# Gelu split into four operations, and P.V accumulated in PSUM with the score fill ahead of it

## The chip, the cores and the metric

The kernel runs on one core of one Trainium2 chip. Its engines are TensorE (PE in the profile; its weight loads are PEld), VectorE (DVE), ScalarE (ACT), GpSimd (POOL) and SyncE (SP), which here only issues DMAs. Each runs its own list of instructions in order, and the lists are tied together by semaphores: an instruction waits until a counter has reached a value. The metric is the time of one execution on the device in microseconds; lower is better.

## The reference

Input is one sequence of S = 2048 rows and D = 512 columns in bf16. Four residual blocks follow each other, with the same weights for both of a kind: A, B, A, B, each on the layernorm of x.

```
A: q = (x @ wq) as 32 heads of 16; k = x @ wk; v = x @ wv     # one k and v for all heads
   p = softmax(q k^T / 4);  o = p v;  out = concat(o) @ wo
B: z = gelu_tanh(x @ w_in)                                     # 1792 wide
   z1 = z[..., :896];  z2 = layernorm(z[..., 896:])
   g = w_sp @ z2 + b_sp                                        # 2048 x 2048 mixing of rows
   out = (z1 * g) @ w_out
x = x + A(ln(x));  x = x + B(ln(x));  x = x + A(ln(x));  x = x + B(ln(x))
```

gelu_tanh(u) is 0.5 u (1 + tanh(0.798 u + 0.0357 u^3)).

## The kernel before

x stays in SBUF (tile `X`) through all four layers. All the instructions are put into one list per engine by `K.op(engine, fn, waits, inc)`, in the order in which the Python code calls it; that order is the only scheduler there is. The waits given to one call stand in front of that instruction, so what comes later on that engine is queued behind them.

**Start** (lines 182 to 246). SP issues the loads of x (four), wq, wk, wv, wo (semaphore wA), then w_in and w_out (wB) and b_sp. DVE zeroes and fills padded copies of wq, wk and wv, sets `V_aug` to zero with a column of ones per head slot (that column gives the softmax denominator), and then starts the first layernorm (`bn_stats` L275, `bn_aggr` L276).

**Layer A** (`layer_A`). Work is cut into units: (qc, hg, kt) is one chunk of 512 query rows, one group of four heads and one tile of 128 keys. There are 4 x 8 x 16 = 512 units; the 16 units of one (qc, hg) are called a group. A unit has four blocks, one per head, of 128 keys x 512 queries. Three blocks at a time form a fill: `emit_fill(i)` puts three score matmuls (L754) into three of six PSUM banks, and `emit_exp(i)` (L773) lets ScalarE take exp of all three banks in one instruction of 128x1536 into `P_ring`, a ring of 12 blocks. So there are 683 exps in a layer. `emit_pv(u)` (L793) multiplies four blocks of `P_ring` with `V_aug` into one bank, `pv_bank`, each head into its own 32 partitions. In the kernel before, every unit's product is complete in itself, and DVE adds it into `acc_sb` in SBUF: a copy for the first of a group (L814), adds for the next 14 (L816), and the last add writes `oT_bf` (L818). P.V of the next unit waits for that add, since there is one bank.

Beside it runs a list of side tasks that share one bank, one per step of the main loop: layernorm transposes and K/V projections at the start, 30 Q projections (L487) and, in layer 0, 32 tasks that transpose w_sp; after each group a finalize task (four transposes of `oT_bf`, L663, then a reciprocal and a scaling on DVE, L668 and L673); after each query chunk two transposing tasks into `onT` (L697) and four Wo tasks (L715), which add to `X` (L720). `emit_side_pe` puts the next task's TensorE part into the list, and `emit_side_dve` its DVE part.

**Layer B** (`layer_B`). After layernorm and transposes, 60 items go through TensorE: first 32 for z2 (16 row tiles x 2 halves of 448 columns, L899), then 28 for z1 (four chunks x seven tiles of 128x512, L904), each four matmuls into one of four banks (`slot = k % 4`). `step_gelu` turns each bank with one `Gelu_apprx_tanh` on ScalarE (L933) into bf16 in `z2n` or `z1c`. For z2, DVE takes `bn_stats` (L937) and `bn_aggr` (L940) and, six items later, normalizes the row tile in place (L952); POOL computes the reciprocal root (L941, L943). Then per chunk of 512 rows: the mixing matmuls (L1009) read all of `z2n`, DVE adds b_sp (L1019) and multiplies with z1 (L1025), and the last matmuls with `w_out_r` (L1041) are added to `X` (L1047).

Of the kernel before, what the change touches and what calls it, by code (L numbers as in the profile page):

```python
# [5 lines left out]
FP32 = mybir.dt.float32  # L6
BF16 = mybir.dt.bfloat16
# [10 lines left out]
NF1 = 7  # L18
# [86 lines left out]
def bass_interleave_layers__grouped_kv_mqa__mixer_gmlp__prompt_kernel(  # L105
# [89 lines left out]
    with ExitStack() as wst:  # L195
# [23 lines left out]
        def dve_memset(ap, val, waits=()):  # L219
            return K.op("dve", lambda e: e.memset(ap, val), waits=waits, inc=S_dve)  # L220
# [19 lines left out]
                wv_rep[:].rearrange("p kd (g r) -> p kd g r", r=32)[:, :, :, 0:DH],  # L240
                wv_nat[:, :, None, :].to_broadcast([P, KD, 4, DH])),
            waits=[(S_dve, v0), wA], inc=S_dve)
        v0 = dve_memset(V_aug[:], 0.0)
        w_prep_v = dve_memset(V_aug[:].rearrange("p t (c r) -> p t c r", r=32)[:, :, :, DH], 1.0,
                              waits=[(S_dve, v0)])
# [86 lines left out]
    def layer_A(layer_idx, x_waits, do_wspt=False):  # L332
# [9 lines left out]
        acc_sb = K.sb([P, QC], FP32, lst, name="acc_sb")  # L342
# [435 lines left out]
        def emit_pv(u):  # L778
            qc, hg, kt = units[u]
            kc = kt // CT  # L780
            while kc not in V_ready:
                progressed = emit_side_pe()
                progressed = emit_side_dve() or progressed
                assert progressed, "V block task missing"
            wl = [(S_exp, exp_base + iu(u) + 1), V_ready[kc], prologue_done]
            if u >= 1:
                wl.append((S_acc, acc_base + u))

            def pe_fn(e):
                ins = None  # L790
                for j in range(4):
                    slot = (4 * u + j) % 12
                    ins = e.matmul(pv_bank[32 * j:32 * j + 32, 0:QC], V_aug[:, kt, 32 * j:32 * j + 32], P_ring[:, slot, :],  # L793
                                   tile_position=(0, 32 * j), start=True, stop=True)
                return ins
            K.op("pe", pe_fn, waits=wl, inc=S_pv)

        def emit_acc(u):
            qc, hg, kt = units[u]
            grp = u // NT  # L800
            par = grp % 2
            wl = [(S_pv, pv_base + u + 1)]
            if u >= 1:
                wl.append((S_acc, acc_base + u))
            last = (kt == NT - 1)
            if last and grp >= 2:
# [4 lines left out]
            if NT == 1:  # L811
                fn = lambda e: e.tensor_copy(oT_bf[:, par, :], pv_bank[:, 0:QC])
            elif kt == 0:
                fn = lambda e: e.tensor_copy(acc_sb[:], pv_bank[:, 0:QC])  # L814
            elif not last:
                fn = lambda e: e.tensor_tensor(acc_sb[:], pv_bank[:, 0:QC], acc_sb[:], ALU.add)  # L816
            else:
                fn = lambda e: e.tensor_tensor(oT_bf[:, par, :], pv_bank[:, 0:QC], acc_sb[:], ALU.add)  # L818
            v = K.op("dve", fn, waits=wl, inc=S_acc)
            if last:  # L820
                side_urgent.append(make_fin_task(qc, hg, par, v))
                if hg == 7:
                    qpar = qc % 2
                    nhalf = (NQT + 1) // 2
                    for half in range(nhalf):
                        side_urgent.append(make_ont_task(qc, half, qpar))
                    for qt in range(NQT):
                        side_urgent.append(make_wo_task(qc, qt, qpar))

        pending_pv = {}  # L830
        for u in range(U):
# [3 lines left out]
            emit_fill(1)  # L835
        for i in range(NI):
            emit_exp(i)
            for u in pending_pv.get(i, []):
                emit_pv(u)
                emit_acc(u)  # L840
            if i + 2 < NI:
                emit_fill(i + 2)
            emit_side_pe(allow_bg=(i % SIDE_PERIOD == 0))
            emit_side_dve()
        for i in range(NI, NI + 8):
            for u in pending_pv.get(i, []):
                emit_pv(u)
                emit_acc(u)
# [12 lines left out]
    def layer_B(layer_idx, x_waits):  # L861
# [12 lines left out]
        z2n = K.sb([P, NT, FH], BF16, lst, name="z2n")  # L874
        z1c = K.sb([P, NF1, S], BF16, lst, name="z1c")
        NSLOT = 4
        st2 = K.sb([P, NT, 2, 6], FP32, lst, name="st2")
        mv2 = K.sb([P, NT, 2], FP32, lst, name="mv2")
        veps2 = K.sb([P, NT], FP32, lst, name="veps2")
        rstd2 = K.sb([P, NT], FP32, lst, name="rstd2")  # L880

        items = []
        for t in range(NT):
# [28 lines left out]
            _, tc, ft = it  # L912
            return z1c[:, ft, tc * TCW:(tc + 1) * TCW]

        st = {"pe": [None] * NIT, "a0": [None] * NIT}
# [11 lines left out]
        def step_gelu(k):  # L927
            it = items[k]
            slot = k % NSLOT
            bk = bank32(slot)  # L930
            n = item_N(it)
            oap = out_ap(it)
            st["a0"][k] = K.op("act", lambda e, bk=bk, n=n, oap=oap: e.activation(  # L933
                oap, bk[:, 0:n], ACTF.Gelu_apprx_tanh), waits=[(S_pe, st["pe"][k])], inc=S_act)
            if it[0] == "z2":
                _, t, h = it
                v1 = K.op("dve", lambda e, t=t, h=h: e.bn_stats(st2[:, t, h, :], z2n[:, t, h * 448:(h + 1) * 448]),  # L937
                          waits=[(S_act, st["a0"][k])], inc=(S_dloc if h == 1 else None))
                if h == 1:
                    vm[t] = K.op("dve", lambda e, t=t: e.bn_aggr(mv2[:, t, :], st2[:, t, :, :]), waits=[(S_dloc, v1)], inc=S_dve)  # L940
                    vp1 = K.op("pool", lambda e, t=t: e.tensor_scalar(veps2[:, t:t + 1], mv2[:, t, 1:2], LN_EPS, None,  # L941
                                                                       op0=ALU.add), waits=[(S_dve, vm[t])], inc=S_ploc)
# [25 lines left out]
        z2n_all = (S_dve, max(vz2n))  # L968
# [16 lines left out]
        for tc in range(NTC):  # L985
# [9 lines left out]
            for ft in range(NF1):  # L995
# [8 lines left out]
                def pe_g(e, ft=ft, bk=bk, wb=wb, first_g=first_g):  # L1004
                    ins = None
                    for sti in range(NT):
                        if first_g:
                            e.wait_ge(S_dve.h, vz2n[sti])
                        ins = e.matmul(bk[:, 0:TCW], z2n[:, sti, ft * 128:(ft + 1) * 128], wspT[:, wb, sti, :],  # L1009
                                       start=(sti == 0), stop=(sti == NT - 1))  # L1010
                    return ins
                if first_g:
                    wl = [w_ for w_ in wl if w_ is not z2n_all]
                    K.waited["pe"][id(S_dve)] = max(K.waited["pe"].get(id(S_dve), 0), vz2n[NT - 1])
# [15 lines left out]
            for tt in range(NTT):  # L1030
                t = tc * NTT + tt
                yb = tt % 2
                bk = bank32(6 + yb)
                wl = [(S_dve, vh[NF1 - 1]), w_prep, wB]
                if y_bank_free[yb] is not None:
                    wl.append((S_dve, y_bank_free[yb]))

# [60 lines left out]
```

## Time and profile before

| | us |
|---|---|
| median of 9 runs | 2534.62 (2532.68 to 2535.91) |
| the profiled execution | 2536.26 |
| its span, first to last instruction | 2534.2 |
| busy: PE, ACT, DVE, POOL | 1875.5, 1983.3, 1096.0, 48.5 |
| exps of layer 0, first start to last end | 46.1 to 1045.6 |
| first MLP, gelu stage (L899, L904) to first mixing matmul | 1095.9 to 1147.5 |
| exps of layer 2 | 1307.4 to 2301.8 |
| second MLP, the same stage | 2352.0 to 2403.7 |

A timeline line gives start, duration, engine, source line, operation, output<-input, shapes and how often it follows itself; in brackets stands how long the engine was idle before it and what ended that. Independent instructions on one engine overlap a little, so that the distance between two starts is less than a duration. Busy PE is not PE at its peak: TensorE's clock is gated, and the column PEclk (or the seventh column of the windows) tells what share of it was granted. A line of the windows gives, for one stretch, its length and then busy time and count for PE, PEld, DVE, ACT and POOL, the clock, the DMA share and GB/s.

### The profile page before, as it was taken

The page shows a single profiled execution, that of the slowest core. Times are in us where ns is not written, and L with a number is a line of the kernel's source. Part 1 is how long each engine was busy: PE and PEld are TensorE (multiplying, and loading weights), DVE is VectorE, ACT ScalarE, POOL GpSimd, SP SyncE. Part 2 cuts the span into 40 slices and gives each one's busy share as a digit, 9 for nine tenths or more (in the row PEclk, how much of TensorE's full clock was granted, in tenths as well). Part 3 has the DMA queues.
Part 4 walks back from the last instruction along what each step waited for, and adds up shares of the span by engine and source line. Part 5 has one row for each costly group of instructions (what it writes and reads, how often), then busy time and mean ns, then how long its engine had stood idle before and what let it go on. Part 6 is the DMA issues. An engine that isn't in the chain of part 4 may idle for free.

```text
span 2534.2 us, 29104 instructions
## 1 busy us (share of the span) xinstructions
PE 1875.5 (74%) x11232; PEld 547.5 (22%) x11232; DVE 1096.0 (43%) x1818; ACT 1983.3 (78%) x1490; POOL 48.5 (2%) x95
## 2 busy tenths in 40 slices
PE   3878777777777777579958777777777777774899
PEld 1223111111111111144422111111111111111444
DVE  5665433343334333463366434333433343334533
ACT  2999999999999999540039999999999999993500
POOL 0000000000000000020000000000000000000200
PEclk9986555555555555589979655555555555555999
DMA  3035000000000000201100000000000000002020
GB/s 119 1 90 152 9 1 1 1 1 1 1 1 1 1 1 1 67 1 34 34 0 1 1 1 1 1 1 1 1 1 1 1 1 1 1 1 66 1 83 17
DMA packets 60088, 43.98 MB, mean 17 GB/s; under 512 B 34864, under 2 KB 57264, under 8 KB 59952
## 3 DMA queue, kind: packets, MB, share of 16 engines
q1 hardware_dynamic: 59952, 42.11, 5.6%
q8 instruction: 92, 1.51, 0.2%
q14 instruction: 44, 0.36, 0.0%
HBM read 31.62 MB, written 10.49 MB: 17 GB/s over the span
## 4 chain that ended last, share of the span: by engine, by line
PE 49%; DVE 21%; ACT 21%; issue 8%; POOL 1%; DMA 0%; SPq 0%; ACTq 0%; DVEq 0%
PE ps_all L793 21%; ACT P_ring L773 21%; DVE acc_sb L816 14%; PE ps_all L1009 8%; PE ps_all L754 7%; PE ps_all L899 2%; PE ps_all L1041 2%; PE ps_all L904 2%; PE ps_all L715 2%; DVE ln_stats L275 2%; DVE oT_bf L818 1%; PE ps_all L663 1%; DVE acc_sb L814 1%; PE ps_all L301 1%; PE ps_all L487 1%
## 5 line engine op out<-in xcount | busy, mean ns | idle before, releaser
L773 ACT ACTIVATE P_ring<-ps_all 128x1536 bf16<-128x1536 f32 (+1 forms) x1366 | 1910.0, 1452 | 286.6 <-PE ps_all L754 254.9
L816 DVE TENSOR_TENSOR acc_sb<-ps_all,acc_sb 128x512 f32<-128x512 f32 x896 | 618.4, 690 | 910.2 <-PE ps_all L793 908.9
L793 PE MATMUL ps_all<-P_ring,V_aug 128*32 128x512 bf16 x4096 | 595.9, 569 | 464.9 <-ACT P_ring L773 258.6
L754 PE MATMUL ps_all<-qT_pad,kT_rep 32*128 32x512 bf16 x4096 | 779.1, 568 | 27.2 <-ACT P_ring L773 13.3
L793 PEld LDWEIGHTS ps_all<-P_ring,V_aug 128*32 128x32 bf16 x4096 | 128.6, 100 | 925.8 <-ACT P_ring L773 888.7
L754 PEld LDWEIGHTS ps_all<-qT_pad,kT_rep 32*128 32x128 bf16 x4096 | 141.2, 98 | 581.1 <-issue 416.4
L1009 PE MATMUL ps_all<-wspT,z2n 128*128 128x512 bf16 x896 | 194.7, 379 | 1.5 <-issue 1.5
L933 ACT ACTIVATE z2n<-ps_all 128x448 bf16<-128x448 f32 x64 | 34.8, 543 | 117.8 <-PE ps_all L899 117.8
L1009 PEld LDWEIGHTS ps_all<-wspT,z2n 128*128 128x128 bf16 x896 | 87.5, 98 | 107.7 <-issue 2.4
L1019 DVE TENSOR_TENSOR gtmp<-ps_all,bsp_bc 128x512 f32<-128x512 f32 x56 | 38.7, 692 | 160.3 <-PE ps_all L1009 160.3
L818 DVE TENSOR_TENSOR oT_bf<-ps_all,acc_sb 128x512 bf16<-128x512 f32 x64 | 44.2, 691 | 69.6 <-PE ps_all L793 69.5
L487 PE MATMUL ps_all<-xnTA,wq_pad 128*128 128x512 bf16 x240 | 63.1, 386 | 1.7 <-DVE o_norm L673 1.3
L492 DVE CAST qT_pad<-ps_all 128x512 bf16<-128x512 f32 x60 | 41.5, 691 | 47.0 <-PE ps_all L487 47.0
L1041 PE MATMUL ps_all<-w_out_r,hT 128*128 128x512 bf16 x224 | 49.7, 379 | 12.1 <-DVE hT L1025 12.1
L899 PE MATMUL ps_all<-w_in_r,xnTB 128*128 128x448 bf16 x256 | 53.5, 375 | 1.6 <-DVE xnTB L309 1.6
L715 PE MATMUL ps_all<-wo_r,onT 128*128 128x512 bf16 x128 | 45.2, 491 | 10.2 <-DVE X L720 6.6
L663 PE MATMUL ps_all<-ident,oT_bf 128*128 128x128 bf16 x256 | 37.5, 298 | 20.0 <-DVE oT_bf L818 20.0
L301 PE MATMUL ps_all<-ident,xnB 128*128 128x128 bf16 x128 | 15.1, 312 | 49.8 <-DVE xnB L290 49.8
L904 PE MATMUL ps_all<-xnTB,w_in_r 128*128 128x512 bf16 x224 | 48.7, 379 | 0.0
L814 DVE COPY acc_sb<-ps_all 128x512 f32<-128x512 f32 x64 | 43.7, 682 | 9.2 <-PE ps_all L793 9.0
L280 POOL TENSOR_SCALAR ln_veps<-ln_mv 128x4 f32<-128x4 f32 (+1 forms) x12 | 2.8, 234 | 2292.9 <-DVE ln_mv L276 2292.9
L933 ACT ACTIVATE z1c<-ps_all 128x512 bf16<-128x512 f32 x56 | 33.4, 597 | 15.0 <-PE ps_all L904 15.0
(59 smaller groups left out, 656.8 us busy)
## 6 DMA issues: line engine op xcount, KB each, us to landing
wspT<-wspt_scratch SPq DMA_DIRECT2D x8, 2048.0 KB, 8.0
wsp_stage<-in_B_w_sp_dram SPq DMA_DIRECT2D x16, 512.0 KB, 3.9
wspt_scratch<-wspT_tile SPq DMA_DIRECT2D x16, 512.0 KB, 5.0
X<-in_A_x_dram SPq DMA_DIRECT2D x4, 512.0 KB, 5.7
out_dram<-X SPq DMA_DIRECT2D x16, 128.0 KB, 3.3
w_in_r<-in_B_w_in_dram SPq DMA_DIRECT2D x1, 1792.0 KB, 9.6
w_out_r<-in_B_w_out_dram SPq DMA_DIRECT2D x1, 896.0 KB, 10.9
wq_nat<-in_A_wq_dram SPq DMA_DIRECT2D x1, 512.0 KB, 8.0
```

The lines of the kernel that those rows point to most:

```text
L487: ins = e.matmul(side_bank32[:, 0:QC], wq_pad[:, kd, hg, :], xnT[:, kd, qc * QC:(qc + 1) * QC], start=(kd == 0), stop=(kd == KD - 1))
L715: ins = e.matmul(side_bank32[:, 0:D], onT[:, par, c, qt * 128:(qt + 1) * 128], wo_r[:, c, :], start=(c == 0), stop=(c == 3))
L754: ins = e.matmul(bk[:, 0:QC], kT_rep[32 * j:32 * j + 32, kt * 128:(kt + 1) * 128], qT_pad[32 * j:32 * j + 32, hg, qc * QC:(qc + 1) * QC], ...
L773: return e.activation(P_ring[:, s0:s0 + n, :], bank32(b0, n).rearrange("p (k q) -> p k q", k=n)[:, :, 0:QC], ACTF.Exp, scale=DH ** -0.5)
L793: ins = e.matmul(pv_bank[32 * j:32 * j + 32, 0:QC], V_aug[:, kt, 32 * j:32 * j + 32], P_ring[:, slot, :], tile_position=(0, 32 * j), start ...
L814: fn = lambda e: e.tensor_copy(acc_sb[:], pv_bank[:, 0:QC])
L816: fn = lambda e: e.tensor_tensor(acc_sb[:], pv_bank[:, 0:QC], acc_sb[:], ALU.add)
L818: fn = lambda e: e.tensor_tensor(oT_bf[:, par, :], pv_bank[:, 0:QC], acc_sb[:], ALU.add)
L899: ins = e.matmul(bk[:, 0:448], xnT[:, kd, t * 128:(t + 1) * 128], w_in_r[:, kd, FH + h * 448:FH + (h + 1) * 448], start=(kd == 0), stop=(k ...
L904: ins = e.matmul(bk[:, 0:TCW], w_in_r[:, kd, ft * 128:(ft + 1) * 128], xnT[:, kd, tc * TCW:(tc + 1) * TCW], start=(kd == 0), stop=(kd == K ...
L1009: ins = e.matmul(bk[:, 0:TCW], z2n[:, sti, ft * 128:(ft + 1) * 128], wspT[:, wb, sti, :], start=(sti == 0), stop=(sti == NT - 1))
L1041: ins = e.matmul(bk[:, 0:D], hT2[:, ft, tt * 128:(tt + 1) * 128], w_out_r[:, ft, :], start=(ft == 0), stop=(ft == NF1 - 1))
```

## The change

In layer A the four P.V matmuls of a unit no longer start afresh: the first unit of a group starts the sums in PSUM, the last one stops them, and DVE copies the bank to `oT_bf` once per group (`emit_evac`). `acc_sb` is gone, and P.V waits for DVE only at the first unit of a group. In the main loop the fill of step i+2 is put into TensorE's list ahead of P.V of step i.

In layer B the single gelu becomes four operations on two engines, in a software pipeline over the items: a0 is Square with a scale on ScalarE, from the bank into `ybuf` (fp32); d3 on DVE makes (square + 0.798) x bank; a1 is Tanh on ScalarE into `thbuf`; d4 on DVE makes (tanh + 1) x bank into `z2n` or `z1c`. That is twice gelu. For z2 the layernorm takes the factor out again with an epsilon of 4e-5; for z1, `w_out_r` is multiplied by 0.5 once at the start, on DVE, after both weights of B have landed. The bank is free for TensorE after d4. The normalization of z2 moves from DVE to ScalarE (Identity with a scale and a bias per row), with a small new DVE operation for the bias (`nb2`).

```diff
@@ start, ahead of V_aug's memset @@
+        K.op("dve", lambda e: e.tensor_scalar(w_out_r[:], w_out_r[:], 0.5, None, op0=ALU.mult),
+             waits=[wB], inc=S_dve)
         v0 = dve_memset(V_aug[:], 0.0)
@@ emit_pv @@
-            if u >= 1:
-                wl.append((S_acc, acc_base + u))
+            first = (kt == 0)
+            last = (kt == NT - 1)
+            grp = u // NT
+            if first and grp >= 1:
+                wl.append((S_acc, acc_base + grp))
...
-                                   tile_position=(0, 32 * j), start=True, stop=True)
+                                   tile_position=(0, 32 * j), start=first, stop=last)
...
+            if last:
+                emit_evac(u)
+
-        def emit_acc(u):
+        def emit_evac(u):
...
-            elif kt == 0:
-                fn = lambda e: e.tensor_copy(acc_sb[:], pv_bank[:, 0:QC])
-            elif not last:
-                fn = lambda e: e.tensor_tensor(acc_sb[:], pv_bank[:, 0:QC], acc_sb[:], ALU.add)
-            else:
-                fn = lambda e: e.tensor_tensor(oT_bf[:, par, :], pv_bank[:, 0:QC], acc_sb[:], ALU.add)
-            v = K.op("dve", fn, waits=wl, inc=S_acc)
+            v = K.op("dve", lambda e: e.tensor_copy(oT_bf[:, par, :], pv_bank[:, 0:QC]), waits=wl, inc=S_acc)
+            side_urgent.append(make_fin_task(qc, hg, par, v))
@@ main loop of layer A @@
             emit_exp(i)
+            if i + 2 < NI:
+                emit_fill(i + 2)
             for u in pending_pv.get(i, []):
                 emit_pv(u)
-                emit_acc(u)
-            if i + 2 < NI:
-                emit_fill(i + 2)
             emit_side_pe(allow_bg=(i % SIDE_PERIOD == 0))
             emit_side_dve()
@@ layer_B: step_pe, step_gelu @@
             if k >= NSLOT:
-                wl.append((S_act, st["a0"][k - NSLOT]))
+                wl.append((S_dve, st["d4"][k - NSLOT]))
...
-            st["a0"][k] = K.op("act", lambda e, bk=bk, n=n, oap=oap: e.activation(
-                oap, bk[:, 0:n], ACTF.Gelu_apprx_tanh), waits=[(S_pe, st["pe"][k])], inc=S_act)
+            st["a0"][k] = K.op("act", lambda e, slot=slot, bk=bk, n=n: e.activation(
+                ybuf[:, slot, 0:n], bk[:, 0:n], ACTF.Square, scale=SQA), waits=wl, inc=S_act)
...
+            st["d3"][k] = K.op("dve", lambda e, slot=slot, bk=bk, n=n: e.scalar_tensor_tensor(
+                ybuf[:, slot, 0:n], ybuf[:, slot, 0:n], GELU_C, bk[:, 0:n], op0=ALU.add, op1=ALU.mult),
+                waits=wl, inc=S_dve)
...
+            st["a1"][k] = K.op("act", lambda e, slot=slot, n=n: e.activation(
+                thbuf[:, slot, 0:n], ybuf[:, slot, 0:n], ACTF.Tanh), waits=wl, inc=S_act)
...
+            st["d4"][k] = K.op("dve", lambda e, slot=slot, bk=bk, n=n, oap=oap: e.scalar_tensor_tensor(
+                oap, thbuf[:, slot, 0:n], 1.0, bk[:, 0:n], op0=ALU.add, op1=ALU.mult),
+                waits=wl, inc=S_dve)
@@ emit_norm @@
-            vz2n[t] = K.op("dve", lambda e, t=t: e.tensor_scalar(z2n[:, t, :], z2n[:, t, :], mv2[:, t, 0:1], rstd2[:, t:t + 1],
-                                                                op0=ALU.subtract, op1=ALU.mult),
-                           waits=[(S_pool, vr2[t]), (S_dve, vm[t])], inc=S_dve)
+            vnb = K.op("dve", lambda e, t=t: e.scalar_tensor_tensor(nb2[:, t:t + 1], mv2[:, t, 0:1], -1.0, rstd2[:, t:t + 1],
+                                                                  op0=ALU.mult, op1=ALU.mult),
+                       waits=[(S_pool, vr2[t])], inc=S_dve)
+            vz2n[t] = K.op("act", lambda e, t=t: e.activation(z2n[:, t, :], z2n[:, t, :], ACTF.Identity,
+                                                              bias=nb2[:, t:t + 1], scale=rstd2[:, t:t + 1]),
+                            waits=[(S_dve, vnb)], inc=S_act)
@@ item loop of layer_B @@
-        for k in range(NIT + 2):
+        LAG = [0, 1, 2, 3, 4]
+        for it_k in range(NIT + 5):
+            k = it_k
             while pending_norm and pending_norm[0][0] <= k:
                 emit_norm(pending_norm.pop(0)[1])
-            if k < NIT:
-                step_pe(k)
-            if 0 <= k - 1 < NIT:
-                step_gelu(k - 1)
-        gelu_done = (S_act, st["a0"][NIT - 1])
+            if 0 <= k - LAG[4] < NIT:
+                step_d4(k - LAG[4])
+            if 0 <= k - LAG[3] < NIT:
+                step_a1(k - LAG[3])
+            if 0 <= k - LAG[2] < NIT:
+                step_d3(k - LAG[2])
+            if 0 <= k - LAG[1] < NIT:
+                step_a0(k - LAG[1])
+            if k - LAG[0] < NIT and k - LAG[0] >= 0:
+                step_pe(k - LAG[0])
+        gelu_done = (S_dve, st["d4"][NIT - 1])
```

More of the change, by code (lines that the diff above doesn't have):

```diff
@@ L341, in layer_A @@
         P_ring = K.sb([P, 12, QC], BF16, lst, name="P_ring")
-        acc_sb = K.sb([P, QC], FP32, lst, name="acc_sb")
         oT_bf = K.sb([P, 2, QC], BF16, lst, name="oT_bf")
@@ L802, in emit_acc @@
             wl = [(S_pv, pv_base + u + 1)]
[L803 to L806, printed above, removed]
+            if grp >= 2:
                 while fin_pe_grp[par] != grp - 2:
@@ L810, in emit_acc @@
                 wl.append((S_spe, fin_pe_val[par]))
-            if NT == 1:
-                fn = lambda e: e.tensor_copy(oT_bf[:, par, :], pv_bank[:, 0:QC])
-            elif kt == 0:
-                fn = lambda e: e.tensor_copy(acc_sb[:], pv_bank[:, 0:QC])
-            elif not last:
-                fn = lambda e: e.tensor_tensor(acc_sb[:], pv_bank[:, 0:QC], acc_sb[:], ALU.add)
-            else:
-                fn = lambda e: e.tensor_tensor(oT_bf[:, par, :], pv_bank[:, 0:QC], acc_sb[:], ALU.add)
-            v = K.op("dve", fn, waits=wl, inc=S_acc)
[L820 to L828, printed above, removed]
+            v = K.op("dve", lambda e: e.tensor_copy(oT_bf[:, par, :], pv_bank[:, 0:QC]), waits=wl, inc=S_acc)
+            side_urgent.append(make_fin_task(qc, hg, par, v))
+            if hg == 7:
+                qpar = qc % 2
+                nhalf = (NQT + 1) // 2
+                for half in range(nhalf):
+                    side_urgent.append(make_ont_task(qc, half, qpar))
+                for qt in range(NQT):
+                    side_urgent.append(make_wo_task(qc, qt, qpar))
         pending_pv = {}
@@ L847, in layer_A @@
                 emit_pv(u)
-                emit_acc(u)
         while side_pending() or side_state["k_dve"] < len(side_emitted):
@@ L876, in layer_B @@
         NSLOT = 4
+        ybuf = K.sb([P, NSLOT, 512], FP32, lst, name="ybuf")
+        thbuf = K.sb([P, NSLOT, 512], BF16, lst, name="thbuf")
         st2 = K.sb([P, NT, 2, 6], FP32, lst, name="st2")
@@ L880, in layer_B @@
         rstd2 = K.sb([P, NT], FP32, lst, name="rstd2")
+        nb2 = K.sb([P, NT], FP32, lst, name="nb2")
         items = []
@@ L913, in out_ap @@
             return z1c[:, ft, tc * TCW:(tc + 1) * TCW]
-        st = {"pe": [None] * NIT, "a0": [None] * NIT}
+        st = {"pe": [None] * NIT, "a0": [None] * NIT, "d3": [None] * NIT, "a1": [None] * NIT, "d4": [None] * NIT}
         vm = [None] * NT
@@ L923, in step_pe, with step_a0 @@
             if k >= NSLOT:
-                wl.append((S_act, st["a0"][k - NSLOT]))
+                assert st["d4"][k - NSLOT] is not None
+                wl.append((S_dve, st["d4"][k - NSLOT]))
             st["pe"][k] = K.op("pe", lambda e, it=it, bk=bk: pe_item(e, it, bk), waits=wl, inc=S_pe)
-        def step_gelu(k):
+        def step_a0(k):
             it = items[k]
@@ L931, in step_gelu, with step_d3, step_a1, step_d4 @@
             n = item_N(it)
+            wl = [(S_pe, st["pe"][k])]
+            if k >= NSLOT:
+                wl.append((S_dve, st["d3"][k - NSLOT]))
+                wl.append((S_act, st["a1"][k - NSLOT]))
+            st["a0"][k] = K.op("act", lambda e, slot=slot, bk=bk, n=n: e.activation(
+                ybuf[:, slot, 0:n], bk[:, 0:n], ACTF.Square, scale=SQA), waits=wl, inc=S_act)
+        def step_d3(k):
+            it = items[k]
+            slot = k % NSLOT
+            bk = bank32(slot)
+            n = item_N(it)
+            wl = [(S_act, st["a0"][k])]
+            st["d3"][k] = K.op("dve", lambda e, slot=slot, bk=bk, n=n: e.scalar_tensor_tensor(
+                ybuf[:, slot, 0:n], ybuf[:, slot, 0:n], GELU_C, bk[:, 0:n], op0=ALU.add, op1=ALU.mult),
+                waits=wl, inc=S_dve)
+        def step_a1(k):
+            it = items[k]
+            slot = k % NSLOT
+            n = item_N(it)
+            wl = [(S_dve, st["d3"][k])]
+            if k >= NSLOT:
+                wl.append((S_dve, st["d4"][k - NSLOT]))
+            st["a1"][k] = K.op("act", lambda e, slot=slot, n=n: e.activation(
+                thbuf[:, slot, 0:n], ybuf[:, slot, 0:n], ACTF.Tanh), waits=wl, inc=S_act)
+        def step_d4(k):
+            it = items[k]
+            slot = k % NSLOT
+            bk = bank32(slot)
+            n = item_N(it)
+            wl = [(S_act, st["a1"][k])]
             oap = out_ap(it)
-            st["a0"][k] = K.op("act", lambda e, bk=bk, n=n, oap=oap: e.activation(
-                oap, bk[:, 0:n], ACTF.Gelu_apprx_tanh), waits=[(S_pe, st["pe"][k])], inc=S_act)
+            st["d4"][k] = K.op("dve", lambda e, slot=slot, bk=bk, n=n, oap=oap: e.scalar_tensor_tensor(
+                oap, thbuf[:, slot, 0:n], 1.0, bk[:, 0:n], op0=ALU.add, op1=ALU.mult),
+                waits=wl, inc=S_dve)
             if it[0] == "z2":
@@ L937, in step_gelu @@
                 v1 = K.op("dve", lambda e, t=t, h=h: e.bn_stats(st2[:, t, h, :], z2n[:, t, h * 448:(h + 1) * 448]),
-                          waits=[(S_act, st["a0"][k])], inc=(S_dloc if h == 1 else None))
+                          waits=[(S_dve, st["d4"][k])], inc=(S_dloc if h == 1 else None))
                 if h == 1:
                     vm[t] = K.op("dve", lambda e, t=t: e.bn_aggr(mv2[:, t, :], st2[:, t, :, :]), waits=[(S_dloc, v1)], inc=S_dve)
-                    vp1 = K.op("pool", lambda e, t=t: e.tensor_scalar(veps2[:, t:t + 1], mv2[:, t, 1:2], LN_EPS, None,
+                    vp1 = K.op("pool", lambda e, t=t: e.tensor_scalar(veps2[:, t:t + 1], mv2[:, t, 1:2], 4.0 * LN_EPS, None,
                                                                        op0=ALU.add), waits=[(S_dve, vm[t])], inc=S_ploc)
@@ L967, in layer_B @@
             emit_norm(pending_norm.pop(0)[1])
-        z2n_all = (S_dve, max(vz2n))
+        z2n_all = (S_act, max(vz2n))
         wspT = K.sb([P, 2, NT, TCW], BF16, lst, name="wspT")
@@ L1007, in pe_g @@
                         if first_g:
-                            e.wait_ge(S_dve.h, vz2n[sti])
+                            e.wait_ge(S_act.h, vz2n[sti])
                         ins = e.matmul(bk[:, 0:TCW], z2n[:, sti, ft * 128:(ft + 1) * 128], wspT[:, wb, sti, :],
@@ L1013, in layer_B @@
                     wl = [w_ for w_ in wl if w_ is not z2n_all]
-                    K.waited["pe"][id(S_dve)] = max(K.waited["pe"].get(id(S_dve), 0), vz2n[NT - 1])
+                    K.waited["pe"][id(S_act)] = max(K.waited["pe"].get(id(S_act), 0), vz2n[NT - 1])
                 vg = K.op("pe", pe_g, waits=wl, inc=S_pe)
@@ L1033, in layer_B @@
                 bk = bank32(6 + yb)
-                wl = [(S_dve, vh[NF1 - 1]), w_prep, wB]
+                wl = [(S_dve, vh[NF1 - 1]), w_prep]
                 if y_bank_free[yb] is not None:
```

## The prediction

> **What bounds the kernel now.** I read the page first (busy time, the 40 slices), then the timeline of one stretch of attention, ScalarE's own timeline, the chain through one MLP, and windows of the clock.
>
> ```profile
> PE 1875.5 (74%) x11232; PEld 547.5 (22%) x11232; DVE 1096.0 (43%) x1818; ACT 1983.3 (78%) x1490; POOL 48.5 (2%) x95
> ...
> ACT  2999999999999999540039999999999999993500
> ...
> PEclk9986555555555555589979655555555555555999
> ```
>
> Two attention layers (ACT slices at 9) hold about 2,000 of 2,534 us; the MLPs (slices of ACT below 6, PE at 9) hold the rest. In attention ScalarE looks full, but its own timeline shows two paces for the same exp (128x1536, 1.452 us each on the page):
>
> ```profile
> 1334.39 10.85 ACT L773 ACTIVATE P_ring<-ps_all 128x1536 bf16<-128x1536 f32 x8 [0.17 <-PE ps_all L754]
> 1345.61 56.70 ACT L773 ACTIVATE P_ring<-ps_all 128x1536 bf16<-128x1536 f32 x42 [0.37 <-PE ps_all L754]
> ```
> ```profile
> 645.63 30.12 ACT L773 ACTIVATE P_ring<-ps_all 128x1536 bf16<-128x1536 f32 x21 [0.51 <-PE ps_all L754]
> 676.25 61.36 ACT L773 ACTIVATE P_ring<-ps_all 128x1536 bf16<-128x1536 f32 x43 [0.50 <-PE ps_all L754]
> 738.12 30.12 ACT L773 ACTIVATE P_ring<-ps_all 128x1536 bf16<-128x1536 f32 x21 [0.51 <-PE ps_all L754]
> ```
>
> Early, at full clock, 42 exps in a row take 56.70 us, so they start (56.70-1.45)/41 = 1.35 us apart. In the steady stretch at half clock it is (61.36-1.45)/42 = 1.43, and with the 0.5 us stalls 64 exps (three head groups) take 738.12-645.63 = 92.49 us. So ScalarE is not at its own pace; who holds it shows in the timeline of one unit:
>
> ```profile
> 701.32 0.69 DVE L816 TENSOR_TENSOR acc_sb<-ps_all,acc_sb 128x512 f32<-128x512 f32 x1 [2.02 <-PE ps_all L793]
> 702.12 0.14 PEld L793 LDWEIGHTS ps_all<-P_ring,V_aug 128*32 128x32 bf16 x4 [0.83 <-ACT P_ring L773]
> 702.15 0.62 PE L793 MATMUL ps_all<-P_ring,V_aug 128*32 128x512 bf16 x4 [0.35 <-DVE acc_sb L816]
> ...
> 702.71 0.61 PE L754 MATMUL ps_all<-qT_pad,kT_rep 32*128 32x512 bf16 x3
> 702.82 0.69 DVE L816 TENSOR_TENSOR acc_sb<-ps_all,acc_sb 128x512 f32<-128x512 f32 x1 [0.81 <-PE ps_all L793]
> ```
>
> P.V waits 0.14 us after DVE's add (701.32+0.69), the next add starts 0.67 after P.V: a loop of 1.51 us a unit. The score fill that feeds the exp after next stands behind P.V, so two of every four exps are released late.
>
> The MLP is TensorE's: its two matmul lines touch each other in the chain, gelu lies beside them.
>
> ```profile
> 1095.86 26.78 PE ps_all L899 x128
> 1122.63 24.17 PE ps_all L904 x112
> ...
> 1147.54 24.35 PE ps_all L1009 x112
> ```
>
> **Change part 1: P.V accumulates in PSUM, fill first.** It removes 15 of 16 adds of a group (896 L816 and 64 L814 of 0.69 us) from DVE, and the wait of P.V on them. After an exp ends, PE issues the fill at once. From the rows at half clock: P.V to the next instruction is 0.56 (702.15 to 702.71), fill to exp 0.65 (702.71+0.61+0.04), fill plus P.V about 1.1 a step, under 1.35, with one step in four having no P.V. The fill is ready some 0.4 us before ScalarE wants it, so I take 1.35 an exp. What is late next is the group end: the finalize transposes stand right behind the last P.V and wait for its evacuation:
>
> ```profile
> 704.32 0.69 DVE L818 TENSOR_TENSOR oT_bf<-ps_all,acc_sb 128x512 bf16<-128x512 f32 x1 [0.81 <-PE ps_all L793]
> ...
> 705.07 0.61 PE L663 MATMUL ps_all<-ident,oT_bf 128*128 128x128 bf16 x4 [0.25 <-DVE oT_bf L818]
> ```
>
> Now a fill covers most of that evacuation; afterwards nothing does. Queued behind it are the next fill, and the exp that waits for it. Counted from the end of an exp: fill 0.54, P.V to evacuation 0.67, evacuation 0.69, transposes start 0.06 later and hold PE 0.54, fill to exp 0.65: 3.15 us. That exp is wanted 3x1.35 after the first one's start, which is 4.05-1.50 = 2.55 after its end (1.45 of exp and 0.05 of signal). So 0.6 us a group is lost. 64 exps then take 86.4+1.8 = 88.2 against 92.5: 4.3 won. About 540 exps of layer 0 and 600 of layer 2 (683 each) run steadily at half clock; less 7 at each of three chunk ends a layer that is 1,100/64 = 17 times 4.3 = 74 us. At the six chunk ends (two onT and four Wo tasks in a row) PE itself is full; the fin wait and tasks in order cost there some 1.5 us more than now: +10. In the early stretches (projections and transposes beside attention) exps already come at 1.35 to 1.5: -6. Sum -70. Bounds: 1,366 exps at 1.35 end to end are 1,844 us, while the two layers' exps now span 999.5 and 994.3: at most -150. Other end: stalls at group ends and in PE's queue eat all, 0.
>
> **Part 2: gelu in four operations.** An item (half a z2 tile, or one z1 tile) had one gelu (543 or 597 ns on ScalarE); now Square and Tanh there, two scalar_tensor_tensor on DVE, and PE's bank is free only after the fourth. The new operations aren't in the trace; nearest rows: DVE with PSUM source 128x512 f32 0.69 (L816, L1019), so 0.62 at 448; the gelu rows for Square and Tanh, 0.54. Independent DVE instructions overlap by 0.10, dependent ones follow after 0.04:
>
> ```profile
> 38.60 1.28 DVE L309 COPY xnTA<-ps_all 128x1024 bf16<-128x1024 bf16 x2
> ```
>
> (2x0.69-0.10). DVE for a z2 item: fourth step 0.62+0.04, bn_stats 0.62-0.09, third step 0.62-0.09: 1.72; each second item adds bn_aggr 0.25 (208 ns on the page) and nb2 0.06. So 3.76 a pair, 32 items 60.2 us. ScalarE has 4x0.45 plus the norm that moves to it (896 elements: 0.92 by the slope between the 448 and the 1536 rows), 2.7 a pair: hidden behind DVE. PE, even at half clock (first 12 matmuls 4.66 us, 1.55 an item), is hidden too. z1: DVE 2x0.60 = 1.20, PE 24.17/28 = 0.86 at full clock, 1.75 at half. Which clock? Windows of about 3.4 us:
>
> ```profile
> 554.40:557.82 3.42, 3.42 (x14) 0.79 (x12) 1.29 (x2) 1.65 (x2) 0.00 (x0) 0.50 0.00 0
> 557.82:561.23 3.41, 3.14 (x22) 0.92 (x21) 2.39 (x4) 2.14 (x3) 0.00 (x0) 0.97 0.00 0
> ...
> 564.64:568.06 3.42, 1.36 (x14) 0.40 (x14) 0.98 (x2) 3.42 (x4) 0.00 (x0) 1.00 0.00 0
> 568.06:571.47 3.41, 2.60 (x21) 0.56 (x17) 1.52 (x3) 3.41 (x3) 0.00 (x0) 0.53 0.00 0
> ```
>
> A window that PE fills at half clock brings full clock; one with 1.36 of 3.42 busy loses it. z2 at DVE's pace would be 0.76 (0.86x448/512) of 1.88 at full clock: it falls to half. z1 starts at half, fills PE, rises, and is then 0.86 of 1.20: I take 3 items at 1.75 and 25 at 1.4, 40 us (bounds 34 and 49). Start-up and fill of the chain 3.3 (first bn_stats now 2.3 after the first matmul, plus a step). Stage: 60.2+40+3.3 = 103.5 against 1147.54-1095.86 = 51.7: +51.8; the next stage (L1009) starts at half clock, +1.7. Twice: +107. Bounds: +89 (z1 at 34, no clock loss) to +145 (no overlap on DVE: 69 for z2; z1 49; 3 for the clock).
>
> The Trainium skill (TensorE: Matmul & The Clock Gate, Why this matters for your kernels) says no gap over some 3 us between matmuls is needed to keep full clock. The window at 564.64 had no such gap and lost it, so the measurement decides; by the rule z1 would be 34 and the sum 16 us lower.
>
> **Part 3: w_out halved at the start.** The multiply waits on DVE for both MLP weights. Behind it in DVE's queue stand the V_aug memset and the whole first layernorm, on which TensorE waits.
>
> ```profile
> 14.89 0.23 DVE L239 COPY wv_rep<-wv_nat 128x256 bf16<-128x256 bf16 x1
> 15.28 0.91 DVE L220 MEMSET V_aug<- 128x1024 uint32 x1 [0.16 <-issue]
> ```
>
> w_out is issued at 9.68 and lands 10.9 later, 20.6; the multiply (128x3584 bf16, by the 2048 copy's 0.69 and the 896 row's 0.475) is 1.0. V_aug starts at 21.6 in place of 15.3: +6.3 (0 if covered, 7 at most).
>
> **Sum.** -70+107+6 = +43 on the profiled execution's 2536.3 (span 2534.2); that is 1.6 above the median of 9, so 2534.6+43 = 2578.
>
> **The rivals.**
> - *Faster:* PE holds full clock through attention. Then fill 0.33, P.V 0.33 and transposes shrink, the group-end exp is ready at about 2.3 after that end instead of 3.15, and no stall is left there: the -150 above less some 3 at each chunk end, -130; sum -17, 2518. It decides where a window stays above some 0.7 busy; demand at full clock is (4x0.33+3x0.33)/5.4 = 0.43, which speaks against.
> - *Attention gives nothing:* 1.43 stays the steady pace, only stalls move. 2534.6+113 = 2648. The 1.35 runs speak against.
> - *MLP dearer:* nothing overlaps on DVE, z1 at half clock, attention -40: +145+6-40, 2646.
> - *Tables:* if Square and Tanh alternate with a table load each (1.283 us in L773 and L933), an item costs ScalarE 2.57+1.1+0.4: 4.1x60-104 = +142 a layer more, 2862. The trace shows loads at stage changes alone, four in all.
>
> The skill (ScalarE: Activation LUTs, Table sets) lists tanh in exp's set and doesn't name Square there; no row here shows either.
>
> **How the numbers follow.** Forecast (2,545 to 2,615) 0.75; faster rival 0.07; nothing from attention 0.08; dear MLP 0.07; tables 0.03. A part of the forecast's low tail and of the faster rival falls within 0.2% of 2534.6 (5 us, about what can be told): same 0.03, faster 0.06, slower 0.91. The range 2,543 to 2,640 leaves out the faster case, the tables and some 0.1 of the two near 2,647, 0.2 in all.
>
> **What would show it.** Exps at 1.35 with one stall near 0.6 at every group end; no acc_sb; DVE near full and PE clock near 0.5 in the first MLP stage, 60 us for z2; V_aug memset at 21.6; no table load in the MLP. Wrong if the steady exp pace stays at 1.43, or z2 items take other than 1.9 us.

## The result, and the profile after

The changed kernel takes 2545.14 us (median of 11 runs, 2543.38 to 2548.03) against 2534.89 for the kernel before (33 runs): a ratio of 1.0042, 95% interval 1.0034 to 1.005. It is 10 us slower, where +43 was forecast. The profiled execution's span is 2544.1 us, 9.9 longer than that of before.

The page of the changed kernel, its engines and three rows of the 40 slices:

```profile
PE 1896.0 (75%) x11232; PEld 522.9 (21%) x11232; DVE 576.9 (23%) x1099; ACT 2004.3 (79%) x1639; POOL 43.9 (2%) x95
...
DVE  4322100010001000794352101000100000018933
ACT  1999999999999998280039999999999999964700
...
PEclk9987555555555555699979655555555555556999
```

DVE's total has halved (1096.0 to 576.9): the adds of attention are gone, and its busy slices are now the MLPs. The attention slices (ACT at 9) end earlier.

ScalarE's timeline in a steady stretch of layer 0, which answers to the lines at 645.63 to 738.12 before:

```profile
653.98 28.31 ACT L774 ACTIVATE P_ring<-ps_all 128x1536 bf16<-128x1536 f32 x21 [0.53 <-PE ps_all L755]
682.82 29.66 ACT L774 ACTIVATE P_ring<-ps_all 128x1536 bf16<-128x1536 f32 x22 [0.53 <-PE ps_all L755]
713.01 28.32 ACT L774 ACTIVATE P_ring<-ps_all 128x1536 bf16<-128x1536 f32 x21 [0.53 <-PE ps_all L755]
741.85 28.32 ACT L774 ACTIVATE P_ring<-ps_all 128x1536 bf16<-128x1536 f32 x21 [0.53 <-PE ps_all L755]
```

Three head groups, 64 exps, now take 741.85-653.98 = 87.87 us in place of 92.49, and each group ends in exactly one gap. What makes that gap is seen in the timeline of one group's end:

```profile
680.20 0.62 PE L797 MATMUL ps_all<-P_ring,V_aug 128*32 128x512 bf16 x4
680.88 0.69 DVE L814 CAST oT_bf<-ps_all 128x512 bf16<-128x512 f32 x1 [26.73 <-PE ps_all L797]
...
681.62 0.61 PE L664 MATMUL ps_all<-ident,oT_bf 128*128 128x128 bf16 x4 [0.80 <-DVE oT_bf L814]
...
682.16 0.79 PE L755 MATMUL ps_all<-qT_pad,kT_rep 32*128 32x512 bf16 x4
```

TensorE stands 0.80 us for the evacuation, and the fill at 682.16, whose exp starts at 682.82, is queued behind it.

DVE's timeline over a z2 item in the first MLP (the fourth step, bn_stats, the third step, the bias of the norm, the next fourth step):

```profile
1074.43 0.62 DVE L962 SCALAR_TENSOR_TENSOR z2n<-thbuf,ps_all 128x448 bf16<-128x448 bf16 x1
1075.08 0.63 DVE L967 BATCH_NORM_STATS2 st<-z2n 128x6 f32<-128x448 bf16 x1
1075.62 0.60 DVE L941 SCALAR_TENSOR_TENSOR ybuf<-ybuf,ps_all 128x448 f32<-128x448 f32 x1
1076.14 0.15 DVE L982 SCALAR_TENSOR_TENSOR nb<-mv,rstd 128x1 f32<-128x1 f32 x1
1076.21 0.61 DVE L962 SCALAR_TENSOR_TENSOR z2n<-thbuf,ps_all 128x448 bf16<-128x448 bf16 x1
```

No idle time stands in brackets: DVE goes from one to the next, which points to it as what sets the pace, and c2 below tests that. And at the start, DVE's timeline:

```profile
20.18 1.09 DVE L243 TENSOR_SCALAR w_out_r<-w_out_r 128x3584 bf16<-128x3584 bf16 x1 [5.31 <-DMA w_out_r<-in_B_w_out_dram]
21.43 0.91 DVE L220 MEMSET V_aug<- 128x1024 uint32 x1 [0.16 <-issue]
```

Where the 9.9 us come from, from the starts of the exps and of the first matmuls of each stage in the two traces:

| part | forecast | measured | how |
|---|---|---|---|
| start | +6.3 | +6.5 | first exp at 46.1, then at 52.6 |
| steady exps, 1,096 of both layers | -74 | -79.3 | 1.447 us an exp, then 1.375 |
| six chunk ends, 8 exps each | +10 | +0.6 | 86.8, then 87.4 |
| early stretches (141 and 79 exps) | -6 | -9.4 | 319.1, then 309.7 |
| gelu stage, two layers | +103.6 | +90.5 | 51.7, then 96.9 each |
| the rest (next stage's clock, borders) | +3.4 | +1.0 | difference to the whole |
| sum | +43 | +9.9 | |

The early stretches are the least certain row: in the profiles of c1 to c4 below, whose layer A is the same there, they take 305.9 to 307.7 us.

### The profile page after: what moved, and what is told of

Its sections match the earlier page's. It is cut to its first block, busy times and chain, and to the rows that moved or that the text cites. A ratio compares the mean times of both kernels' runs of the same rounds, so it can differ in the third digit from the quotient of the medians.

```text
span 2544.1 us, 26634 instructions
## 1 busy us (share of the span) xinstructions
PE 1896.0 (75%) x11232; PEld 522.9 (21%) x11232; DVE 576.9 (23%) x1099; ACT 2004.3 (79%) x1639; POOL 43.9 (2%) x95
## 4 chain that ended last, share of the span: by engine, by line
issue 34%; ACT 28%; PE 23%; DVE 14%; POOL 1%; DMA 0%; SPq 0%; ACTq 0%
ACT P_ring L774 28%; PE ps_all L1050 8%; PE ps_all L755 4%; DVE ybuf L941 2%; PE ps_all L797 2%; PE ps_all L1082 2%; PE ps_all L716 2%; DVE oT_bf L814 2%; DVE st L967 2%; DVE ln_stats L277 2%; PE ps_all L664 1%; DVE z2n L962 1%; DVE z1c L962 1%; PE ps_all L303 1%; DVE X L721 1%
## 5 line engine op out<-in xcount | busy, mean ns | idle before, releaser
L774 ACT ACTIVATE P_ring<-ps_all 128x1536 bf16<-128x1536 f32 (+1 forms) x1366 | 1846.9, 1554 | 270.8 <-PE ps_all L755 270.3
L814 DVE CAST oT_bf<-ps_all 128x512 bf16<-128x512 f32 x64 | 44.3, 692 | 1422.9 <-PE ps_all L797 1422.7
L797 PEld LDWEIGHTS ps_all<-P_ring,V_aug 128*32 128x32 bf16 x4096 | 112.1, 100 | 417.6 <-issue 413.5
L932 ACT ACTIVATE ybuf<-ps_all 128x448 f32<-128x448 f32 (+1 forms) x120 | 66.1, 551 | 105.5 <-PE ps_all L894 105.5
L894 PE MATMUL ps_all<-w_in_r,xnTB 128*128 128x448 bf16 x256 | 72.8, 423 | 40.2 <-DVE z2n L962 38.0
L941 DVE SCALAR_TENSOR_TENSOR ybuf<-ybuf,ps_all 128x448 f32<-128x448 f32 (+1 forms) x120 | 75.8, 632 | 6.4 <-ACT ybuf L932 6.4
L952 ACT ACTIVATE thbuf<-ybuf 128x448 bf16<-128x448 f32 (+1 forms) x120 | 71.2, 593 | 6.6 <-DVE ybuf L941 3.0
L899 PE MATMUL ps_all<-xnTB,w_in_r 128*128 128x512 bf16 x224 | 58.1, 382 | 17.5 <-DVE z1c L962 10.7
L985 ACT ACTIVATE z2n<-z2n,nb,rstd 128x896 bf16<-128x896 bf16 x32 | 36.2, 1133 | 23.4 <-DVE nb L982 23.2
L277 DVE BATCH_NORM_STATS2 ln_stats<-X 128x6 f32<-128x512 bf16 x64 | 42.5, 664 | 0.2
```

Source lines behind the costliest of these rows:

```text
L277: v1 = K.op("dve", lambda e, t=t: e.bn_stats(ln_stats[:, t, :], X[:, t, :]), waits=xw_for(xw, t), inc=S_dloc)
L774: return e.activation(P_ring[:, s0:s0 + n, :], bank32(b0, n).rearrange("p (k q) -> p k q", k=n)[:, :, 0:QC], ACTF.Exp, scale=DH ** -0.5)
L814: v = K.op("dve", lambda e: e.tensor_copy(oT_bf[:, par, :], pv_bank[:, 0:QC]), waits=wl, inc=S_acc)
L894: ins = e.matmul(bk[:, 0:448], xnT[:, kd, t * 128:(t + 1) * 128], w_in_r[:, kd, FH + h * 448:FH + (h + 1) * 448], start=(kd == 0), stop=(k ...
L932: st["a0"][k] = K.op("act", lambda e, slot=slot, bk=bk, n=n: e.activation(ybuf[:, slot, 0:n], bk[:, 0:n], ACTF.Square, scale=SQA), waits=w ...
L941: st["d3"][k] = K.op("dve", lambda e, slot=slot, bk=bk, n=n: e.scalar_tensor_tensor(ybuf[:, slot, 0:n], ybuf[:, slot, 0:n], GELU_C, bk[:, ...
```

## The experiments

**The two layers apart.** Theory: the two parts of the change don't touch each other, so they add up. Rival: one helps the other (DVE free in attention, tables no longer swapped).

```diff
a1_attention_alone: layer_A as changed; layer_B as before; no multiply of w_out
a2_mlp_alone:       layer_A as before;  layer_B as changed; multiply of w_out at the start
```

> Layer A of the changed kernel with layer B of the kernel before, and no multiply of w_out. If the parts of the change just add up: the two exp stretches are 953 us each as in the changed kernel (46 and 41 shorter), nothing else moves: about 2446 us. If the parts lean on each other (layer B's new form helping layer A), it is above 2460.

Measured: 2442.16 us, ratio to before 0.9628 (0.961 to 0.9646).

> Layer A of the kernel before with layer B of the changed kernel and the multiply of w_out. If the parts add up: 6.5 us at the start and 45.2 + 1.5 us for each layer B: about 2634 us.

Measured: 2632.14 us, ratio 1.0375 (1.0354 to 1.0395); its gelu stage is 96.9 us in both layers, as in the changed kernel. The ratios multiply to 0.9989 and the changed kernel has 1.0042, so the parts add up to within half a per cent: attention wins nearly 4%, the MLP loses nearly 4%, and what the whole does is the small difference of the two. The half per cent left over is some 13 us, more than the 10 us of the whole, so this sum can't give the whole's sign; the equal gelu stages are the stronger evidence that the parts don't lean on each other.

**Which half of the attention change wins.** It does two things to the same loop: it takes the add away, and it takes the fill out from behind P.V.

```diff
a3_accumulate_only (on a1_attention_alone)
-            if i + 2 < NI:
-                emit_fill(i + 2)
             for u in pending_pv.get(i, []):
                 emit_pv(u)
+            if i + 2 < NI:
+                emit_fill(i + 2)
a4_order_only (on the kernel before)
+            if i + 2 < NI:
+                emit_fill(i + 2)
             for u in pending_pv.get(i, []):
                 emit_pv(u)
                 emit_acc(u)
-            if i + 2 < NI:
-                emit_fill(i + 2)
```

> As a1_attention_alone, but P.V stands ahead of the fill again, so only the accumulation in PSUM is left of the change to layer A. Theory: the loop P.V, add, P.V of 1.51 us was what made the fill late; without it the fill starts 0.57 us after an exp's end and its exp is ready 1.22 us after it, which asks for 1.35 us an exp; group ends cost about 0.5 us each as before: 2445 to 2465 us. Rival, that the order in TensorE's list is what wins: the pace stays at 1.43 us and the time near 2530 us.

> The kernel before with nothing but the fill put ahead of P.V; DVE still adds every unit. Theory: the loop P.V, add, P.V (3 x 1.51 = 4.5 us in 4 exps of 1.33 = 5.3 us) then has room beside the exps, and the fill no longer stands behind it: pace 1.33 to 1.36 us, group ends 0.9 us each: 2445 to 2465 us. Each half of the change to layer A would then be enough alone. Rival, that the loop itself is the limit: near 2530 us.

Measured: 2452.34 us (0.9666, 0.9645 to 0.9686) and 2451.73 us (0.9669, 0.9641 to 0.9697). Either half alone gives all but some 10 us of what both give. In the steady stretches the three means are equal: 1.375 us an exp with both, 1.376 with the accumulation alone, 1.378 with the order alone. (With the accumulation alone the mean is made up otherwise: 1.35 us between exps where the other two have 1.33, and smaller and fewer gaps at group ends.) The timeline of a3, and under it that of a4 (its P.V, fill and add), show the two ways out of the same wait:

```profile
660.87 0.62 PE L795 MATMUL ps_all<-P_ring,V_aug 128*32 128x512 bf16 x4 [0.75 <-ACT P_ring L772]
...
661.42 0.61 PE L753 MATMUL ps_all<-qT_pad,kT_rep 32*128 32x512 bf16 x3
```
```profile
660.64 0.62 PE L793 MATMUL ps_all<-P_ring,V_aug 128*32 128x512 bf16 x4
...
661.31 0.61 PE L754 MATMUL ps_all<-qT_pad,kT_rep 32*128 32x512 bf16 x3
661.31 0.69 DVE L816 TENSOR_TENSOR acc_sb<-ps_all,acc_sb 128x512 f32<-128x512 f32 x1 [0.72 <-PE ps_all L793]
```

In a3 P.V is released by the exp and no longer by the add, and the fill follows 0.55 us after it, early enough. In a4 the add still runs in every unit, with idle time before it: the loop is there and has room. So in the steady stretches the halving of DVE's work is worth nothing beyond what the order alone gives: there the add cost time only because the fill was queued behind the P.V that waited for it. Where the 10 us between either half and both come from was not taken apart, and whether the order alone would also gain from the later finalize of b1 was not run.

**The gap at a group's end.** Theory: TensorE idle for the evacuation, with the next fill behind it. Rival: TensorE simply has too much to do at a group's end.

```diff
b1_finalize_later (on the changed kernel; b2 the same on a1_attention_alone)
-            side_urgent.append(make_fin_task(qc, hg, par, v))
+            side_late.append(make_fin_task(qc, hg, par, v))     # onT and Wo tasks likewise
...
             emit_exp(i)
+            due = list(side_late)
+            side_late.clear()
             ...                                                 # fill i+2, P.V of step i
+            side_urgent.extend(due)
             emit_side_pe(allow_bg=(i % SIDE_PERIOD == 0))
```

> The changed kernel with the side tasks of a group's end (finalize, onT, Wo) given to TensorE one step later, behind the next fill and the next P.V, so that TensorE no longer stands idle for the evacuation. Theory: the 0.9 us that an exp loses at 58 plain group ends goes: about 50 us less than the changed kernel, 2495 us. Rival, that TensorE's total work at a group's end is what is late: no more than 10 us less, 2535 to 2545 us.

Measured: 2504.66 us, 0.9871 (0.9856 to 0.9887), 40 us below the changed kernel. ScalarE's timeline has one line where the changed kernel has four:

```profile
638.59 121.38 ACT L775 ACTIVATE P_ring<-ps_all 128x1536 bf16<-128x1536 f32 x90
```

No gap is left that breaks the line, and the steady pace is 1.340 us an exp. The 1,096 steady exps hold 1,096/21.33 = 51 groups, and (1.375-1.340) x 1,096 = 38 us, so the later finalize won 0.75 us a group. The gap itself had been 0.9 us, as the expectation took it: 55 of the steady exps of the changed kernel start 2.20 us after the one before, the others 1.33. In b1 27 still start 1.64 us after the one before, so a part of the gap stays at about every second group. The eight exps counted at each chunk end did not get shorter (88.0 us in all against 87.4), but they begin just behind the group's own gap. Over fourteen exps at each of the six chunk ends it is 141.7 us in the changed kernel and 136.0 in b1: that gap goes there too, and what onT and Wo cost behind it stays.

> a1_attention_alone with the finalize tasks one step later. If the gains add up: 2446 - 50 = 2396 us, below both kernels.

Measured: 2407.2 us, 0.949 (0.9477 to 0.9503): the fastest kernel here, 5% below the kernel before. It has the gelu of before, the accumulation, the new order and the later finalize.

**The multiply at the start.**

```diff
c1_multiply_later
-        K.op("dve", ... tensor_scalar(w_out_r[:], w_out_r[:], 0.5 ...), waits=[wB])   # at the start
         for i in range(NI):
+            if do_wspt and i == 200:
+                K.op("dve", ... tensor_scalar(w_out_r[:], w_out_r[:], 0.5 ...), waits=[wB])
             emit_exp(i)
```

> The changed kernel with the multiply of w_out by 0.5 put into DVE's list in the middle of layer 0's exps, where DVE is idle. Theory: the start is 6.5 us earlier and nothing takes its place: 2538.5 us. Rival, that the first exp waits for something else as well: 2545 us.

Measured: 2537.74 us (11 runs), 1.0006 (0.9997 to 1.0015). This is 7 us less than the changed kernel and can't be told from the kernel before: the first exp starts at 46.4 us again (46.1 before, 52.6 in the changed kernel), so all of the 6.5 us was DVE's wait for the weights.

**What sets the pace of the gelu stage.**

```diff
c2_norm_on_dve
-            vnb = ...                      # bias on DVE
-            vz2n[t] = K.op("act", ... Identity, bias=nb2, scale=rstd2 ...)
+            vz2n[t] = K.op("dve", ... tensor_scalar(z2n, z2n, mv2, rstd2, subtract, mult) ...)
...                                        # the mixing matmuls then wait for DVE's counter
```

> The changed kernel with the normalization of z2 back on DVE (and no nb2). Theory, DVE sets the pace of the z2 items: each pair of items has 0.48 us more and 0.15 us less on DVE, with overlap +0.3 us, 16 pairs a layer: z2 about 5 us longer a layer, 2555 us. Rival, that ScalarE or TensorE sets it: ScalarE is relieved of 1.13 us a pair, and the time falls below 2545 us.

Measured: 2552.11 us, 1.006 (1.0046 to 1.0074). z2 takes 64.6 us a layer in place of 59.3 (first to 33rd fourth step), 5.3 more as expected, while ScalarE has 1.13 us a pair less. So DVE sets the pace of z2.

```diff
c3_z1_three_tiles (c4_z1_two_tiles: range(2), stop=(kd == 1)); only for z1 items
-                for kd in range(KD):
+                for kd in range(3):
                     ins = e.matmul(bk[:, 0:TCW], w_in_r[:, kd, ...], xnT[:, kd, ...],
-                                   start=(kd == 0), stop=(kd == KD - 1))
+                                   start=(kd == 0), stop=(kd == 2))
```

> The changed kernel with three of the four contraction tiles in each z1 item (the last 128 columns of the layernormed x are left out of z1). TensorE then has 0.65 us in 1.18 at full clock and 1.31 at half. If a window under some 0.65 busy loses the clock, as the prediction took it from attention, z1 falls to half clock for a part of its windows and its items take 1.2 to 1.3 us: the same time or longer with less work. Rival, that DVE's pace holds whatever the clock: 1.18 us an item, stage 96.9 us, total within 2 us of 2545.

> The same with two of four contraction tiles: 0.43 us at full clock, 0.88 at half, both under DVE's 1.18. Items stay at 1.18 us whatever the clock does; z1 loses full clock, so that the mixing matmuls start at half clock: the stage 96.9 us, the first mixing chunk no shorter than the 25.9 us of the changed kernel, total within 4 us of 2545.

Measured, one run each, beside one run of the kernel before at 2530.88 us: 2543.97 and 2545.53 us. Both stages are 96.9 us, and z1's fourth steps come 1.20 us apart in all three kernels (the expectations had 1.18). What counts is the traces; single runs can't tell a few us.

With 3/4 of the work z1 did lose the clock, but only near its start: in the first MLP from 1112.37 to 1119.19 us. Then it ran at full clock to its end. With 2/4 it was at half clock for most of z1, from 1113.94 to 1137.84, and then at full clock again; the first mixing chunk is 25.8 us. Neither changed the items, so the rival of the first expectation held. A window of c3 in its stretch at half clock; then one in the middle of z1, of the changed kernel and under it of c4:

```profile
1115.78:1119.19 3.41, 2.82 (x7) 0.58 (x6) 3.38 (x8) 3.29 (x6) 0.79 (x2) 0.50 0.00 0
```
```profile
1124.80:1128.20 3.40, 2.93 (x13) 0.93 (x12) 3.40 (x7) 3.16 (x7) 0.00 (x0) 1.00 0.00 0
```
```profile
1124.80:1128.20 3.40, 3.02 (x6) 0.39 (x6) 3.40 (x7) 3.16 (x7) 0.00 (x0) 0.50 0.00 0
```

In the middle of z1 the clock is 1.00 in the changed kernel and 0.50 in c4; DVE is busy for 3.40 of 3.40 us in both, with 7 instructions. DVE's pace holds at either clock, as long as TensorE's work fits under it.

With all four tiles z1 met half clock only for a few items. In the second MLP of a2, z1's first matmul starts at 2460.16 us, at half clock, just as the prediction had it:

```profile
2460.20:2463.60 3.40, 3.37 (x8) 0.83 (x8) 3.30 (x9) 2.63 (x6) 0.79 (x2) 0.50 0.00 0
```

TensorE is full there, and the stage is 96.9 us all the same. DVE is still at z2's items then, 1.85 us apart: its first fourth step of z1 comes 6.5 us after z1's first matmul. In c2's first MLP half clock came later, from 1122.12 to 1125.54, with z1 under way and TensorE busy for 3.40 of 3.40 us, and from the first z1 fourth step to the mixing it took 33.4 us where the changed kernel has 33.3. A long stretch of z1 at half clock with all four tiles did not occur; there the 1.75 us an item of the prediction would lie above DVE's 1.20, and that is untested.

## Why the prediction was wrong

The direction was right, but the forecast of +43 us is four times the measured +10. What was forecast for the start, for z2 and for the steady exps came by the mechanism that was given. Two terms of the sum failed: z1 of the gelu stage, 13 of the 33 us, and the chunk ends, 9. The steady exps (5), the early stretches (3) and the rest (2) were off the same way. Attention came to -88 where -70 was forecast, and layer B to +91 where +107 was; the whole is their small difference, so that errors of 15 to 26% made it four times too large.

- *Gelu stage, z1.* The step "z1 starts at half, fills PE, rises, and is then 0.86 of 1.20: I take 3 items at 1.75 and 25 at 1.4, 40 us" failed: it let TensorE's clock set the pace of z1. From the first z1 fourth step to the mixing it was 33.3 us in the changed kernel, DVE's 1.20 an item, which is the lower bound given there. Twice 6.7 is 13.4 us, the largest error. The clock did not start at half: it had risen for good in the middle of z2, at 1100.88 us, and stayed at full with 2.93 of 3.40 us busy in z1. And where z1 did start at half clock (a2, second MLP), it cost nothing.
- *The clock in z2.* It was to fall to half, with the sign "PE clock near 0.5 in the first MLP stage". It was 0.90 on average over that stage: z2 went between full and half clock for some 40 us and then stayed at full.
- *Attention, chunk ends.* The step "the fin wait and tasks in order cost there some 1.5 us more than now: +10" failed: they cost the same (+0.6). TensorE is busy for 74.05 of the 87.40 us there, and for 72.45 of 86.77 before. That its work with the onT and Wo tasks bounds both, so that the wait adds nothing, is argued and not shown by a run.
- *Attention, steady pace.* 87.9 us for 64 exps where 88.2 was worked out, with the one gap at each group's end that was named as what is late next. That the sum is so close is luck: the exps come 1.33 us apart, not 1.35, and the gap is 0.9 us, not 0.6, and the two errors nearly cancel. Over 1,096 exps it came to -79.3 instead of -74. What the step missed is that each of the two edits would have been nearly enough; it told them as one.
- *Early stretches.* -9.4 against -6.
- *Gelu stage, z2 and start-up.* z2 was right: 59.3 us against 60.2, with DVE as the bound. Start-up was 1 us dearer a layer than forecast.
- *The next stage.* Right: the first mixing chunk starts at half clock and takes 25.91 and 25.78 us in place of 24.35, 3.0 in all where 3.4 was forecast. TensorE stands idle for 3.38 us ahead of it.
- *The rule of the Trainium skill that was weighed there* (TensorE: Matmul & The Clock Gate, Why this matters for your kernels: no idle gap of TensorE over some 3 us, so full clock is kept) gave 34 us for z1, which came out. But z2 shows that the rule isn't the whole: full clock was lost there twice in a layer with no gap over 1.0 us.
- *Start.* Right: 6.5 against 6.3, and c1 gives it back.
- *Rivals.* Attention gained more than nothing; PE stayed at half clock through the steady stretches, so the faster rival did not come (the 0.7 busy given for it is no threshold: z2 windows kept full clock at 1.66 of 3.50 us); DVE's instructions did overlap; no table load stands in the MLP (one load in the whole kernel, four before).

## What to carry to other kernels

Look at what is queued behind an instruction that waits, before removing what it waits for: putting the next stage's work ahead of the waiter won as much as taking 15 of 16 adds away. Where a change trades two large terms against each other, price each to a few per cent or give the sum a range that reaches across zero; and where another engine's work fits under the bound at either clock, as in c4, its clock is no term of the sum. When a task waits for the result of the instruction just ahead of it, issue it one step later: that alone was worth 40 us here.

## What the runs showed of the hardware that was not expected

- ScalarE's exp has a mean duration of 1554 ns after and 1452 ns before, and yet the exps come closer together (1.375 against 1.447 us). Consecutive exps overlap more in the trace (where they do, by 0.22 us on average against 0.10), so a longer duration is no slower engine; the distance between starts is what counts.
- The clock did not follow the busy share alone. In z2 windows of the changed kernel full clock was kept after one with 1.66 of 3.50 us busy, went to half after the next with 1.56 of 3.40, and came back after two windows at half clock:

```profile
1066.70:1070.20 3.50, 1.66 (x9) 0.62 (x8) 3.40 (x8) 2.73 (x6) 0.81 (x2) 1.00 0.01 2
1070.20:1073.60 3.40, 1.56 (x9) 0.55 (x8) 3.33 (x8) 2.62 (x5) 0.79 (x2) 1.00 0.00 0
1073.60:1077.00 3.40, 2.71 (x8) 0.67 (x7) 3.30 (x9) 2.62 (x6) 0.79 (x2) 0.50 0.00 0
1077.00:1080.40 3.40, 3.16 (x8) 0.75 (x7) 3.33 (x8) 2.63 (x6) 0.79 (x2) 0.50 0.00 0
1080.40:1083.80 3.40, 1.94 (x9) 0.62 (x8) 3.30 (x9) 2.63 (x6) 0.79 (x2) 1.00 0.00 0
```

  In attention of the same kernel a window with 1.81 of 3.42 us busy, more than those two, was the last at full clock:

```profile
308.98:312.40 3.42, 1.81 (x17) 0.47 (x17) 0.00 (x0) 3.42 (x3) 0.00 (x0) 1.00 0.01 2
```

  The way back does not follow it either: c4's z1 stayed at half clock after windows with 2.9 of 3.4 us busy, and c3's rose after one with 2.82. What the gate counts stays open.
- The norm on ScalarE with a scale and a bias per row (128x896) took 1.13 us, where 0.92 was worked out from operations without them.
